# First head pair of a cluster attention: norms, identity products in TensorE's pauses, transfers and masks rearranged

## The chip, the cores and the metric

The kernel runs on one core of a Trainium2 chip. The metric is the device time of one execution in microseconds (us), as the median of three runs. All times below are in us unless they are marked ns. The engines are called TensorE (PE in the views; PEld is its weight load), VectorE (DVE), ScalarE (ACT), GpSimd (POOL) and SyncE (SP, which here only issues transfers).

## The reference

Attention over 2 batches, 8 heads, 768 positions and 64 elements a head, in which a query sees only the keys of its own cluster; two expert layers follow, which the change does not touch.

```python
def _attn_ref(q, k, v, centroids) -> np.ndarray:
    ...
    q_n = q / (np.linalg.norm(q, axis=-1, keepdims=True) + 1e-06)
    k_n = k / (np.linalg.norm(k, axis=-1, keepdims=True) + 1e-06)
    c_n = centroids / (np.linalg.norm(centroids, axis=-1, keepdims=True) + 1e-06)
    q_assign = np.argmax(np.einsum('bhsd,hcd->bhsc', q_n, c_n), axis=-1)
    k_assign = np.argmax(np.einsum('bhsd,hcd->bhsc', k_n, c_n), axis=-1)
    mask = q_assign[:, :, :, None] == k_assign[:, :, None, :]
    scores = scale * np.matmul(q, k.transpose(0, 1, 3, 2))
    scores = np.where(mask, scores, -1000000000.0)
    scores = scores - np.max(scores, axis=-1, keepdims=True)
    attn = np.exp(scores)
    attn = attn / (np.sum(attn, axis=-1, keepdims=True) + 1e-09)
    return np.matmul(attn, v).astype(np.float32)

def reference(**kwargs):
    ...
    x = _moe_ref(x=x, **moe_kwargs)
    return _moe2_ref(x=x, **moe2_kwargs)
```

## The kernel before

The order of the instructions is written out by hand: each engine works through its queue in the order of the program, and a semaphore holds an instruction until its operands are there.

Heads go in eight pairs. A loop of 96 steps (`s`), 12 to a pair, does the attention: a step takes 128 queries of one head against 768 keys (`st_scores`, score buffer `sps`, one of the two buffers of tag S), reduces the row maximum on VectorE (`st`), takes the exponential on ScalarE (`st_exp`, `pr`), and three steps later transposes `pr` on TensorE (`tps`) and copies it out on ScalarE (`pt`). The preparation of the next pair is spread over the steps by a table (`plan`, `prep`); that of pair 0, and part of that of pair 1, stands ahead of the loop, and the change lies there.

Ahead of the loop, for pair 0:

- `load_qk(0)` loads q and k of the pair into `first`; `first_copy` sorts them into `nat`; `raw_pe` transposes them in four parts (q half 0, q half 1, k half 0, k half 1) into `rawps`, and `raw_act` copies each part to `raw`.
- `prep_centroids` makes the norms of the centroids from `cnat` on VectorE, with a square root on ScalarE and two steps that improve it, and writes the normed centroids `cexp`; `prep_cblk` transposes them (`cps`) and copies them to `cblk`.
- `assign_pe` multiplies `raw` by `cblk` (`asps`), `assign_act` copies the result (`sc`), `argmax_pe` transposes it (`scps`), and `argmax_0` to `argmax_3` find each position's cluster on VectorE (`mx`, `eq`, `eq`, `mx`, `oh`).
- `mask_first` transposes the one-hot clusters `oh` in 24 small pieces (`mps`). ScalarE copies the keys' part and VectorE scales the queries' part into rows 64 to 79 of `UA` (head 0) and `UB` (head 1).
- The scores are made in float32 from two parts of each operand: `first_hi` makes the high part (in `UA`, both heads stacked), `first_lo` the low one. Nine transfers inside the core's memory (192 KB each, L502 to L516) bring the parts of each head together in `UA`, `UB`, `VA` and `VB`. A step multiplies first the U tiles and then the V tiles of its head.

For pair 1, `raw_pe`, `raw_act` and `split_first` do the same from `natq` and `natk`; its splits run on GpSimd.

A product or transpose of TensorE loads its stationary operand first (PEld). A float32 product of `nc.tensor.matmul` is issued as two instructions, a transpose as one. `warm` is a 1-column tile on which ScalarE runs an Sqrt at the start and an Exp before the loop, so that the function tables are loaded there.

Of the kernel before, what the change touches and what calls it, by code (L numbers as in the profile page):

```python
# [25 lines left out]
def kernel(  # L26
# [66 lines left out]
    def load_qk(p):  # L93
        b, cc = divmod(p, NPAIR)
        for nm, src in (("q", q), ("k", k)):
            if p:
                t = att_a.tile([P, NT, 2, D], F32, tag="nat" + nm, name="nat" + nm)
                nat[nm, p] = t
                nc.sync.dma_start(t, src[b, 2 * cc:2 * cc + 2].rearrange("h (p t) d -> p t h d", t=NT))
            else:  # L100
                t = att.tile([P, 2, HS], F32R, tag="pr", name="first", bufs=4)
                t = _f(t.rearrange("p a b -> p (a b)")).rearrange("p (h t d) -> p h t d", h=2, d=D)
                nc.sync.dma_start(t, src[b, 0:2].rearrange("h (p t) d -> p h t d", t=NT))
                first[nm] = t
                nat[nm, 0] = nat0[:, "qk".index(nm)]
            if p == 0 and nm == "q":
                nc.sync.dma_start(cnat, centroids.rearrange("h c d -> (h c) d"))
# [29 lines left out]
    nc.scalar.activation(out=warm, in_=warm, func=AF.Sqrt)  # L137
# [5 lines left out]
    def prep_centroids():  # L143
        sq = att_a.tile([P, D], F32, tag="csq", name="csq")
        st = att_a.tile([P, 8], F32, tag="cst", name="cst")
        nc.vector.tensor_tensor(out=sq, in0=cnat, in1=cnat, op=ALU.mult)
        nc.vector.tensor_reduce(out=st[:, 0:1], in_=sq, axis=AX.X, op=ALU.add)
        first_copy(1)
        nc.scalar.activation(out=st[:, 1:2], in_=st[:, 0:1], func=AF.Sqrt)
        nc.vector.tensor_scalar(out=st[:, 1:2], in0=st[:, 1:2], scalar1=1e-30, scalar2=None, op0=ALU.max)  # L150
        for i in (1, 2):
            nc.vector.reciprocal(out=st[:, 3:4], in_=st[:, i:i + 1])
            nc.vector.scalar_tensor_tensor(out=st[:, 3:4], in0=st[:, 0:1], scalar=st[:, 3:4], in1=st[:, i:i + 1],
                                           op0=ALU.mult, op1=ALU.add)
            nc.vector.tensor_scalar(out=st[:, 2 * i:2 * i + 1], in0=st[:, 3:4], scalar1=0.5, scalar2=1e-6 * (i - 1),
                                    op0=ALU.mult, op1=ALU.add)
        nc.vector.reciprocal(out=st[:, 4:5], in_=st[:, 4:5])
        for h in range(2):
            nc.vector.tensor_scalar(out=cexp[:, h, :], in0=cnat, scalar1=st[:, 4:5], scalar2=par[:, h:h + 1],
                                    op0=ALU.mult, op1=ALU.mult)  # L160

    def prep_cblk():
        cps = ps_s("cps")[:, 0, 0:P]
        nc.tensor.transpose(cps, cexp.rearrange("p h d -> p (h d)"), ident)
        nc.vector.tensor_copy(cblk.rearrange("p a b -> p (a b)"), cps)
# [5 lines left out]
    def raw_pe(p, i):  # L171
# [5 lines left out]
        ps = ((ps_t, ps_t, ps_m, ps_a)[i] if p == 0 else ((ps_t, ps_t, ps_a, ps_t)[i] if p == 1 else ps_m))([P, 3, P], "rawps")  # L177
# [9 lines left out]
    def raw_act(p, i):  # L187
        qk, half = divmod(i, 2)
        ps = ps_prep.pop(("raw", i)).rearrange("p j c -> p (j c)")
        sc = SCALE if qk == 0 else 1.0  # L190
        nc.scalar.activation(out=raw_t[p][:, i, :], in_=ps, func=AF.Copy, scale=sc)
# [9 lines left out]
    def raw_split(p, i):  # L201
# [6 lines left out]
        nc.gpsimd.tensor_scalar(out=hi, in0=raw[:, i, :], scalar1=1.0, scalar2=1.0, op0=ALU.mult, op1=ALU.mult)  # L208
# [63 lines left out]

    def mask_first(h):
        U = uv_t[0][h]
        for qk in (1, 0):
# [8 lines left out]
            else:  # L284
                for cs in (slice(0, HS), slice(HS, S)) if h == 0 else (slice(0, S),):
                    nc.vector.tensor_scalar(out=U[64:64 + NC_, 0, cs], in0=ps[:, cs], scalar1=BIG, scalar2=-BIG,
                                            op0=ALU.mult, op1=ALU.add)
# [181 lines left out]
    def first_copy(i):  # L469
        nm = "qk"[i // 2]  # L470
        ts_ = slice(3 * (i % 2), 3 * (i % 2) + 3)
        for h in range(2):
# [3 lines left out]
            elif nm == "q":  # L476
                nc.vector.tensor_copy(dst, src)
# [3 lines left out]
    first_copy(0)  # L481
    prep_centroids()
    first_copy(2)
    first_copy(3)
    for i in range(4):
        raw_pe(0, i)
        raw_act(0, i)
# [6 lines left out]
    def first_lo(qk, halves=(0, 1)):  # L494
        for half in halves:
# [5 lines left out]
    Uk, Wk, Xk, Yk = (_f(t[:, 1, :]) for t in (UA, UB, VA, VB))  # L501
    nc.sync.dma_start(Wq[0:64], Uq[64:128])  # L502
    nc.sync.dma_start(Yq[64:128], Uq[64:128])
    nc.sync.dma_start(Wk[0:64], Uk[64:128])
    nc.sync.dma_start(Yk[0:64], Uk[64:128])
    first_lo(0, (0,))
    prep_cblk()
    first_lo(0, (1,))
    nc.sync.dma_start(Yq[0:64], Xq[64:128])
    nc.gpsimd.dma_start(Xk[0:64], Uk[0:64])  # L510
    assign_pe(0)
    first_lo(1)
    lo_kf = _f(lo_k.rearrange("p a b -> p (a b)"))
    nc.sync.dma_start(Xk[64:128], lo_kf[0:64])
    nc.sync.dma_start(Yk[64:128], lo_kf[64:128])
    nc.sync.dma_start(Xq[64:128], Uq[0:64])  # L516
    prep(0, 3, "a0")
    nc.scalar.activation(out=warm, in_=warm, func=AF.Exp)
    prep(0, 3, "pb")
    for r in range(4, 7):  # L520
        for slot in ("d", "pb"):
            prep(0, r, slot)
    load_v(0)
    for i in range(4):
        raw_pe(1, i)
        raw_act(1, i)
    load_qk(2)
    mask_first(0)
    mask_first(1)
    for i in range(4):  # L530
# [158 lines left out]
    for s in range(NSTEP + 12 + LAG):  # L689
        p, r = divmod(s, 12)  # L690
        if s < NSTEP:
            st_scores(s)
        conv_step(s, 0)
# [931 lines left out]
```

## Time and profile before

| | |
|---|---|
| median of 3 runs | 644.96 us (644.65 to 645.3) |
| the profiled execution, its own time | 644.19 us |
| its span, first to last instruction | 642.5 us |
| outside its span | 1.7 us |
| TensorE busy in the span | 624.0 us (97%) |
| first product of the loop starts at | 18.61 us |
| mean granted TensorE clock | 0.996 |

The span is the time from the first to the last instruction of one execution that was profiled; what lies outside it is start and end of the program. The profiled execution is 0.77 us shorter than the median of the runs. A busy share is an average over stages with different limits; the stage ahead of the loop has to be read by itself.

### The profile page before, as it was taken

The numbers are of one execution on the slowest core, as the hardware profiler recorded it, in microseconds if no ns is written. First come the engines' busy times: TensorE is split into PE (matmuls) and PEld (weight loads), VectorE is DVE, ScalarE is ACT, GpSimd is POOL, SyncE is SP. The second block draws the span as 40 slices with busy tenths as digits, with TensorE's granted clock in tenths as the row PEclk, the third lists the DMA queues.
The fourth block names the chain that finished last, engine by engine and source line by source line (L and its number), as shares of the span: only waits on it lengthen the run. The fifth ranks groups of instructions, "written<-read, shape, count | busy, mean of one in ns | idle before, by whom it ended". The sixth has DMA issues, their size and how long they took to land.

```text
span 642.5 us, 10035 instructions
## 1 busy us (share of the span) xinstructions
PE 624.0 (97%) x3505; PEld 484.2 (75%) x3505; DVE 484.7 (75%) x893; ACT 417.0 (65%) x817; POOL 164.4 (26%) x215
## 2 busy tenths in 40 slices
PE   5999999999999999999999999999999999999994
PEld 3777777677777775888888888878888778688874
DVE  6757868777878754988865888868887748999961
ACT  5798898988888885655454444435445446688860
POOL 3333647463746333400000000000000125005211
PEclk9999999999999999999999999999999999999998
DMA  7766566578766508132014301008421739999930
GB/s 189 193 180 169 138 153 190 150 197 199 200 186 162 174 31 318 67 119 91 23 36 146 100 33 34 33 2 301 178 94 66 267 137 318 372 363 350 369 135 28
DMA packets 66246, 104.26 MB, mean 162 GB/s; under 512 B 27994, under 2 KB 32060, under 8 KB 65810
## 3 DMA queue, kind: packets, MB, share of 16 engines
q1 hardware_dynamic: 62914, 95.36, 47.5%
q0 software_dynamic: 3280, 8.24, 3.9%
q8 instruction: 28, 0.46, 0.3%
q14 instruction: 24, 0.20, 0.1%
HBM read 77.45 MB, written 12.72 MB: 140 GB/s over the span
## 4 chain that ended last, share of the span: by engine, by line
PE 91%; DVE 3%; ACT 2%; DMA 2%; SPq 1%; issue 1%; POOL 0%; POOLq 0%
PE ups L669 20%; PE acc L775 19%; PE sps L371 10%; PE avps L443 10%; PE tps L428 9%; PE hps L1316 7%; PE yps L1347 7%; PE rawps L179 1%; PE hT L1328 1%; PE acc L1208 1%; PE asps L232 1%; ACT pr L389 1%; DMA stg<-in_moe_w_in_dram 1%; DMA first<-in_k_dram 1%; PE scps L244 1%
## 5 line engine op out<-in xcount | busy, mean ns | idle before, releaser
L374 DVE TENSOR_REDUCE st<-sps 128x1 f32<-128x768 f32 x96 | 91.5, 954 | 49.9 <-PE sps L371 49.1
L435 ACT ACTIVATE pt<-tps 128x384 f32<-128x384 f32 x192 | 85.4, 508 | 17.6 <-PE tps L428 16.4
L389 ACT ACTIVATE pr<-sps,st 128x768 f32<-128x768 f32 x96 | 88.0, 917 | 11.5 <-DVE st L374 11.4
L428 PE MATMUL tps<-ident,pr 128*128 128x128 f32 x576 | 79.0, 273 | 0.5 <-ACT pt L435 0.5
L669 PE MATMUL ups<-xh,whii 128*128 128x512 f32 x192 | 74.9, 390 | 0.0
L669 PE MATMUL ups<-xh,wloi 128*128 128x512 f32 x192 | 74.7, 389 | 0.0
L669 PE MATMUL ups<-xl,whii 128*128 128x512 f32 x192 | 74.7, 389 | 0.0
L428 PEld LDWEIGHTS tps<-ident,pr 128*128 128x128 f32 x576 | 67.9, 140 | 5.6 <-ACT pt L435 1.6
L443 PE MATMUL avps<-pt,vnat 128*64 128x384 f32 x384 | 72.1, 498 | 0.0
L775 PE MATMUL acc<-whio,gh 128*128 128x512 f32 x183 | 72.1, 394 | 0.0
L775 PE MATMUL acc<-whio,gl 128*128 128x512 f32 x183 | 71.3, 389 | 0.0
L775 PE MATMUL acc<-wloo,gh 128*128 128x512 f32 x183 | 71.2, 389 | 0.0
L760 ACT ACTIVATE gh<-g 128x512 fp32r<-128x512 f32 x48 | 30.4, 632 | 47.5 <-DVE g L759 47.5
L758 ACT ACTIVATE lk<-ups 128x512 f32<-128x512 f32 x48 | 28.5, 595 | 48.8 <-PE ups L669 43.4
L762 DVE TENSOR_TENSOR gl<-g,gh 128x512 fp32r<-128x512 f32 x48 | 33.2, 691 | 25.2 <-ACT gh L760 25.2
L1048 POOL DMA_INDIRECT xe<-x_scratch,eix x1 | 1.2, 1165 | 189.8 <-DVE eix L1047 189.8
L881 DVE SCALAR_TENSOR_TENSOR ohe<-x,x2Ts 128x512 f32<-128x512 f32 x63 | 43.4, 689 | 1.5
L443 PEld LDWEIGHTS avps<-pt,vnat 128*64 128x64 f32 x384 | 23.4, 136 | 25.5 <-issue 25.1
L759 DVE TENSOR_TENSOR g<-ups,lk 128x512 f32<-128x512 f32 x48 | 33.0, 688 | 12.7 <-ACT lk L758 12.1
L669 PEld LDWEIGHTS ups<-xh,whii 128*128 128x128 f32 x192 | 36.0, 188 | 8.0 <-issue 0.6
L669 PEld LDWEIGHTS ups<-xh,wloi 128*128 128x128 f32 x192 | 36.0, 188 | 7.5
L669 PEld LDWEIGHTS ups<-xl,whii 128*128 128x128 f32 x192 | 36.1, 188 | 7.4
(312 smaller groups left out, 1367.1 us busy)
## 6 DMA issues: line engine op xcount, KB each, us to landing
rawb<-in_moe_w_dram SPq DMA_DIRECT2D x25, 1024.0 KB
rawa<-in_moe_w_dram SPq DMA_DIRECT2D x10, 1024.0 KB
stg<-in_moe_w_in_dram SPq DMA_DIRECT2D x16, 512.0 KB
stg<-in_moe_w_out_dram SPq DMA_DIRECT2D x16, 512.0 KB
x2Ts<-gate_scratch SPq DMA_DIRECT2D x18, 256.0 KB
UB<-UA SPq DMA_DIRECT2D x16, 192.0 KB
vnat<-in_v_dram SPq DMA_DIRECT2D x8, 384.0 KB
rb<-recip_scratch POOLq DMA_DIRECT2D x32, 96.0 KB, 2.8
```

The lines of the kernel that those rows point to most:

```text
L371: nc.tensor.matmul(ps[:, kh, 0:HS], lhsT=t[0:n, 0, qs], rhs=t[0:n, 1, kh * HS:(kh + 1) * HS], start=first, stop=not first)
L374: nc.vector.tensor_reduce(out=st[:, 0:1], in_=ps[:, :, 0:HS], axis=AX.XY, op=ALU.max, negate=True)
L389: nc.scalar.activation(out=pr, in_=ps[:, :, 0:HS], func=AF.Exp, bias=st[:, 0:1], accum_out=sm_t[g][:, 3 * h + j:3 * h + j + 1])
L428: nc.tensor.transpose(ps[:, t, :], pr[:, kh, t * P:(t + 1) * P], ident)
L435: nc.scalar.activation(out=pt[:, 3 * kh:3 * kh + 3, j, :], in_=t_t[s][kh], func=AF.Copy)
L443: nc.tensor.matmul(av_t[g][64 * h:64 * h + 64, :], lhsT=vnat[p][:, h, kt, :], rhs=pt_t[p, half, h][:, kt].rearrange("p j c -> p (j c)"), s ...
L669: nc.tensor.matmul(ps, lhsT=w[:, cc, :], rhs=x[:, blk, cc, :], start=(n == 0), stop=(n == 3 * KD - 1))
L762: nc.vector.tensor_tensor(out=gl, in0=g, in1=_f(gh), op=ALU.subtract)
L775: nc.tensor.matmul(ps, lhsT=a[:, ts_], rhs=w, start=(fc == 0 and n == 0), stop=(fc == NFC - 1 and n == 2))
L881: nc.vector.scalar_tensor_tensor(out=junk[0].rearrange("p t n -> p (t n)"), in0=x2_t[blk, t // 2][:, t % 2, :], scalar=1.0, in1=wgb_t[blk, ...
L1316: nc.tensor.matmul(ps, lhsT=x[:, c, :], rhs=w, start=(n == 0), stop=(n == len(mm) - 1))
L1347: nc.tensor.matmul(ps[:, cs], lhsT=x[:, f, :], rhs=w[:, cs], start=(h == 0 and f == 0 and n == 0), stop=(h == 1 and f == 3 and n == 2))
```

## The change

The change rewrites the stage ahead of the loop, and the first three steps of the loop.

- The centroids are loaded from ScalarE's queue instead of SP's. The square root of their norms is no longer ScalarE's: VectorE halves the bits of the number as a first guess and takes three improving steps instead of two. The table that ScalarE loads at the start is that of Exp, and the second load before the loop is gone.
- All of `first_copy`'s head-0 part is GpSimd's (VectorE did that of q). The copy of `raw` part 1 is VectorE's instead of ScalarE's.
- `warm_pe(n)` multiplies the identity by itself n times into one half of a score buffer (`first_s`); nobody reads the result. It stands in four places (7, 3, 2 and 6 products). The centroids' transpose uses the other half of the same buffer, and so the three products ahead of `assign_pe` wait for VectorE's copy of it (`cblk`).
- Nine transfers become seven: two parts are copied by ScalarE inside the same partitions (L538, L539 after), and `Xq` is issued from ScalarE's queue instead of SP's, where it stood last.
- Of the queries' masks only half 0 is scaled ahead of the loop; half 1 follows in steps 1 and 2 (`mask_query`).
- Of pair 1, parts 0 and 1 stay ahead of the loop; parts 3 and 2 are transposed and copied after the first step's products. Its splits on GpSimd wait for `hold`, a 1-column tile that VectorE writes behind `oh`.

```diff
-                nc.sync.dma_start(cnat, centroids.rearrange("h c d -> (h c) d"))
+                nc.scalar.dma_start(cnat, centroids.rearrange("h c d -> (h c) d"))
...
-    nc.scalar.activation(out=warm, in_=warm, func=AF.Sqrt)
+    nc.scalar.activation(out=warm, in_=warm, func=AF.Exp)
+    hold = const.tile([P, 1], F32, name="hold")
...
-        first_copy(1)
-        nc.scalar.activation(out=st[:, 1:2], in_=st[:, 0:1], func=AF.Sqrt)
-        nc.vector.tensor_scalar(out=st[:, 1:2], in0=st[:, 1:2], scalar1=1e-30, scalar2=None, op0=ALU.max)
-        for i in (1, 2):
+        si = st.bitcast(I32)
+        nc.vector.tensor_single_scalar(si[:, 1:2], si[:, 0:1], 1, op=ALU.logical_shift_right)
+        nc.vector.tensor_scalar(out=si[:, 1:2], in0=si[:, 1:2], scalar1=float(0x1FBD1DF5), scalar2=None, op0=ALU.add)
+        for i, j in ((1, 2), (2, 5), (5, 4)):
...
+    first_s = ps_s("first")
+
     def prep_cblk():
-        cps = ps_s("cps")[:, 0, 0:P]
+        cps = first_s[:, 1, 0:P]
...
+        if p == 0 and i == 1:
+            nc.vector.tensor_scalar(out=raw_t[p][:, i, :], in0=ps, scalar1=sc, scalar2=None, op0=ALU.mult)
+            return
...
-        nc.gpsimd.tensor_scalar(out=hi, in0=raw[:, i, :], scalar1=1.0, scalar2=1.0, op0=ALU.mult, op1=ALU.mult)
+        nc.gpsimd.tensor_scalar(out=hi, in0=raw[:, i, :], scalar1=hold if p == 1 and i == 0 else 1.0, scalar2=1.0,
+                                op0=ALU.mult, op1=ALU.mult)
...
+    mq_t = {}
+
+    def mask_query(h, half):
+        cs = slice(half * HS, (half + 1) * HS)
+        nc.vector.tensor_scalar(out=uv_t[0][h][64:64 + NC_, 0, cs], in0=mq_t[h][:, cs], scalar1=BIG, scalar2=-BIG,
+                                op0=ALU.mult, op1=ALU.add)
...
-                for cs in (slice(0, HS), slice(HS, S)) if h == 0 else (slice(0, S),):
-                    nc.vector.tensor_scalar(out=U[64:64 + NC_, 0, cs], in0=ps[:, cs], scalar1=BIG, scalar2=-BIG,
-                                            op0=ALU.mult, op1=ALU.add)
+                mq_t[h] = ps
+                mask_query(h, 0)
...
-            elif nm == "q":
-                nc.vector.tensor_copy(dst, src)
...
+    wps = first_s[:, 0, 0:P]
+
+    def warm_pe(n):
+        for _ in range(n):
+            nc.tensor.matmul(wps, lhsT=ident, rhs=ident, start=True, stop=True)
+
+    warm_pe(7)
     prep_centroids()
-    first_copy(2)
-    first_copy(3)
     for i in range(4):
+        first_copy(i)
+    for i in range(3):
         raw_pe(0, i)
-        raw_act(0, i)
+    raw_act(0, 0)
+    raw_act(0, 1)
+    prep_cblk()
+    raw_pe(0, 3)
+    raw_act(0, 2)
+    raw_act(0, 3)
+    warm_pe(3)
+    assign_pe(0)
+    warm_pe(2)
     for i in range(4):
         first_hi(i)
...
     nc.sync.dma_start(Wq[0:64], Uq[64:128])
-    nc.sync.dma_start(Yq[64:128], Uq[64:128])
+    first_lo(0)
+    nc.sync.dma_start(Yq[0:64], Xq[64:128])
     nc.sync.dma_start(Wk[0:64], Uk[64:128])
     nc.sync.dma_start(Yk[0:64], Uk[64:128])
-    first_lo(0, (0,))
-    prep_cblk()
-    first_lo(0, (1,))
-    nc.sync.dma_start(Yq[0:64], Xq[64:128])
-    nc.gpsimd.dma_start(Xk[0:64], Uk[0:64])
-    assign_pe(0)
     first_lo(1)
...
-    nc.sync.dma_start(Xq[64:128], Uq[0:64])
     prep(0, 3, "a0")
-    nc.scalar.activation(out=warm, in_=warm, func=AF.Exp)
     prep(0, 3, "pb")
+    nc.scalar.activation(out=VA[0:64, 1, :], in_=Uk[0:64], func=AF.Copy)
+    nc.scalar.activation(out=VB[64:128, 0, :], in_=Uq[64:128], func=AF.Copy)
+    nc.scalar.dma_start(Xq[64:128], Uq[0:64])
...
-    load_v(0)
-    for i in range(4):
+    nc.vector.memset(hold, 1.0)
+    for i in range(2):
         raw_pe(1, i)
         raw_act(1, i)
+    warm_pe(6)
+    load_v(0)
...
+        if s == 0:
+            for i in (3, 2):
+                raw_pe(1, i)
+            for i in (3, 2):
+                raw_act(1, i)
+            for i in (2, 3):
+                split_first(1, i)
+        if 1 <= s < 3:
+            mask_query(s - 1, 1)
```

Three places of the order. TensorE's queue from its first instruction to the masks (`nat_87` is `nat`, `first` in a product's output is the shared score buffer, `oh` is loaded as the stationary operand of the mask transposes); first before, then after the change:

```order
L179 MATMUL rawps<-ident,nat_87 128x128 x12
L164 MATMUL cps<-ident,cexp 128x128
L232 MATMUL asps<-raw,cblk 32x384 x4
L244 MATMUL scps<-ident,sc 128x128 x3
L179 MATMUL rawps<-ident,natq 128x128 x6
L179 MATMUL rawps<-ident,natk 128x128 x6
L280 LDWEIGHTS oh
```

```order
L496 MATMUL first<-ident 128x128 x7
L182 MATMUL rawps<-ident,nat_87 128x128 x9
L167 MATMUL first<-ident,cexp 128x128
L182 MATMUL rawps<-ident,nat_87 128x128 x3
L496 MATMUL first<-ident 128x128 x3
L239 MATMUL asps<-raw,cblk 32x384 x4
L496 MATMUL first<-ident 128x128 x2
L251 MATMUL scps<-ident,sc 128x128 x3
L182 MATMUL rawps<-ident,natq 128x128 x6
L496 MATMUL first<-ident 128x128 x6
L294 LDWEIGHTS oh
```

Eighteen identity products have come in, the centroids' transpose has moved ahead of the last three transposes of pair 0, and the six transposes of `natk` have left this stretch.

ScalarE's queue from the first copies to the loop's first exponentials (`UA<-mps` and `UB<-mps` are the keys' masks, `pr` the exponentials); first before, then after:

```order
L475 ACTIVATE nat_87<-first 128x3x64 x2
L191 ACTIVATE raw<-rawps 128x384 x4
L197 ACTIVATE UA<-raw 128x384 x2
L238 ACTIVATE sc<-asps 128x384
L518 ACT_TABLE_LOAD
L518 ACTIVATE warm<-warm 128x1
L191 ACTIVATE raw<-rawps 128x384 x4
L283 ACTIVATE UA<-mps 16x768
L283 ACTIVATE UB<-mps 16x768
L389 ACTIVATE pr,sm<-sps,st 128x768 x2
```

```order
L488 ACTIVATE nat_87<-first 128x3x64 x4
L197 ACTIVATE raw<-rawps 128x384 x3
L203 ACTIVATE UA<-raw 128x384 x2
L245 ACTIVATE sc<-asps 128x384
L538 ACTIVATE VA<-UA 64x768
L539 ACTIVATE VB<-UA 64x768
L540 DMA VA<-UA 64x768
L197 ACTIVATE raw<-rawps 128x384 x2
L297 ACTIVATE UA<-mps 16x768
L297 ACTIVATE UB<-mps 16x768
L197 ACTIVATE raw<-rawps 128x384 x2
L402 ACTIVATE pr,sm<-sps,st 128x768 x2
```

One copy of `raw` and the table load have left; two copies of 64 rows and a transfer's issue have come in behind `sc`, and two copies of pair 1 now stand between the masks and the first exponential.

SP's queue from the first transfer inside the core's memory to the loads of `v` and of pair 2; first before, then after:

```order
L502 DMA UB<-UA 64x768
L503 DMA VB<-UA 64x768
L504 DMA UB<-UA 64x768
L505 DMA VB<-UA 64x768
L509 DMA VB<-VA 64x768
L514 DMA VA<-lo_k 64x768
L515 DMA VB<-lo_k 64x768
L516 DMA VA<-UA 64x768
L112 DMA vnat<-in_v_dram 128x2x384
```

```order
L528 DMA UB<-UA 64x768
L530 DMA VB<-VA 64x768
L531 DMA UB<-UA 64x768
L532 DMA VB<-UA 64x768
L534 DMA VA<-lo_k 64x768
L535 DMA VB<-lo_k 64x768
L112 DMA vnat<-in_v_dram 128x2x384
```

The transfer that brings the low part of q (`VB<-VA`) has moved from fifth to second place, and the last one, which may not start before that one has been read, has gone to ScalarE's queue.

## Rows read from the trace of the kernel before

**Rows 1.** Page: busy time by engine; the chain that ended last, by engine.

```profile
PE 624.0 (97%) x3505; PEld 484.2 (75%) x3505; DVE 484.7 (75%) x893; ACT 417.0 (65%) x817; POOL 164.4 (26%) x215
...
PE 91%; DVE 3%; ACT 2%; DMA 2%; SPq 1%; issue 1%; POOL 0%; POOLq 0%
```

**Rows 2.** Chain that ended last, 0 to 20 us: start us, us, what.

```profile
1.81 4.57 DMA first<-in_k_dram
...
9.21 1.57 PE asps L232 x8
...
10.80 0.50 ACT sc L238
...
11.35 0.92 PE scps L244 x3
...
12.29 0.57 DVE mx L251
...
14.65 1.25 DVE oh L269
...
15.95 2.73 PE mps L280 x24
18.68 1.25 PE sps L371 x4
```

**Rows 3.** Timeline, 4 to 10 us: start us, us, engine line operation, count.

```profile
4.03 0.61 ACT L475 ACTIVATE nat<-first 128x192 f32<-128x192 f32 x2 [1.70 <-DMA first<-in_q_dram]
...
4.30 0.21 DVE L146 TENSOR_TENSOR csq<-cnat 128x64 f32<-128x64 f32 x1
...
6.40 0.61 ACT L475 ACTIVATE nat<-first 128x192 f32<-128x192 f32 x2 [1.39 <-DMA first<-in_k_dram]
...
6.71 0.69 DVE L159 TENSOR_SCALAR cexp<-cnat,cst,par 128x64 f32<-128x64 f32 x2
...
6.92 2.03 ACT L191 ACTIVATE raw<-rawps 128x384 f32<-128x384 f32 x4
...
8.79 0.28 DVE L165 COPY cblk<-cps 128x128 f32<-128x128 f32 x1
8.85 0.93 ACT L197 ACTIVATE UA<-raw 128x384 fp32r<-128x384 f32 x2
```

**Rows 4.** Timeline of TensorE later: the same operations, and a 128x128 product.

```profile
20.64 0.85 PE L232 MATMUL asps<-raw,cblk 128*32 128x384 f32 x8
...
23.25 0.55 PE L244 MATMUL scps<-ident,sc 128*128 128x128 f32 x3 [0.29 <-ACT sc L238]
...
31.44 0.33 PE L292 MATMUL ohps<-identb,oh 128*128 128x128 bf16 x3
...
521.21 0.69 PE L1055 MATMUL xT<-ident,xe 128*128 128x128 f32 x4
```

**Rows 5.** Timeline: GpSimd at 15 to 16 us; pair 1's last argmax step.

```profile
15.45 0.81 POOL L208 TENSOR_SCALAR UA<-raw 128x384 fp32r<-128x384 f32 x1
...
30.34 0.55 DVE L269 TENSOR_TENSOR oh<-eq,mx 128x384 bf16<-128x384 f32 x1
```

**Rows 6.** SP's wait, two issues; GpSimd's issue; a window (last: PEclk, DMA, GB/s).

```profile
SPq L516 <- DMA VB<-VA: 1.8, 1, 1.8
...
8.49 0.55 SPq L502 DMA_DIRECT2D UB<-UA  x1
...
16.16 0.46 SPq L516 DMA_DIRECT2D VA<-UA  x1
...
VA<-UA POOLq DMA_DIRECT2D x1, 192.0 KB, 4.6
...
10.00:12.00 2.00, 1.37 (x11) 0.65 (x4) 0.47 (x1) 1.18 (x2) 0.76 (x1) 1.00 0.94 203
```

**Rows 7.** Timeline of ScalarE: the loop's first and fourth exponential.

```profile
20.94 0.90 ACT L389 ACTIVATE pr<-sps,st 128x768 f32<-128x768 f32 x1 [2.07 <-DVE st L374]
...
25.63 0.91 ACT L389 ACTIVATE pr<-sps,st 128x768 f32<-128x768 f32 x1
```

More of the change, by code (lines that the diff above doesn't have):

```diff
@@ L154, in prep_centroids @@
                                            op0=ALU.mult, op1=ALU.add)
-            nc.vector.tensor_scalar(out=st[:, 2 * i:2 * i + 1], in0=st[:, 3:4], scalar1=0.5, scalar2=1e-6 * (i - 1),
+            nc.vector.tensor_scalar(out=st[:, j:j + 1], in0=st[:, 3:4], scalar1=0.5, scalar2=1e-6 if j == 4 else 0.0,
                                     op0=ALU.mult, op1=ALU.add)
@@ L176, in raw_pe @@
         src = nat["qk"[qk], p]
-        ps = ((ps_t, ps_t, ps_m, ps_a)[i] if p == 0 else ((ps_t, ps_t, ps_a, ps_t)[i] if p == 1 else ps_m))([P, 3, P], "rawps")
+        ps = ((ps_t, ps_t, ps_m, ps_a)[i] if p == 0 else ((ps_t, ps_t, ps_m, ps_t)[i] if p == 1 else ps_m))([P, 3, P], "rawps")
         for j in range(3):
@@ L475, in first_copy @@
                 nc.scalar.activation(out=dst, in_=src, func=AF.Copy)
-            elif nm == "q":
-                nc.vector.tensor_copy(dst, src)
             else:
                 nc.gpsimd.tensor_scalar(out=dst, in0=src, scalar1=1.0, scalar2=1.0, op0=ALU.mult, op1=ALU.mult)
-    first_copy(0)
+    wps = first_s[:, 0, 0:P]
[3 more added lines that the diff above has]
+    warm_pe(7)
     prep_centroids()
-    first_copy(2)
-    first_copy(3)
     for i in range(4):
+        first_copy(i)
+    for i in range(3):
         raw_pe(0, i)
-        raw_act(0, i)
+    raw_act(0, 0)
[7 more added lines that the diff above has]
+    warm_pe(2)
     for i in range(4):
@@ L492, with first_lo @@
     lo_k = att.tile([P, 2, HS], F32R, tag="pr", name="lo_k", bufs=4)
-    def first_lo(qk, halves=(0, 1)):
-        for half in halves:
+    def first_lo(qk):
+        for half in range(2):
             cs = slice(half * HS, (half + 1) * HS)
@@ L501 @@
     Uk, Wk, Xk, Yk = (_f(t[:, 1, :]) for t in (UA, UB, VA, VB))
+    lo_kf = _f(lo_k.rearrange("p a b -> p (a b)"))
     nc.sync.dma_start(Wq[0:64], Uq[64:128])
-    nc.sync.dma_start(Yq[64:128], Uq[64:128])
+    first_lo(0)
+    nc.sync.dma_start(Yq[0:64], Xq[64:128])
     nc.sync.dma_start(Wk[0:64], Uk[64:128])
     nc.sync.dma_start(Yk[0:64], Uk[64:128])
-    first_lo(0, (0,))
-    prep_cblk()
-    first_lo(0, (1,))
-    nc.sync.dma_start(Yq[0:64], Xq[64:128])
-    nc.gpsimd.dma_start(Xk[0:64], Uk[0:64])
-    assign_pe(0)
     first_lo(1)
-    lo_kf = _f(lo_k.rearrange("p a b -> p (a b)"))
     nc.sync.dma_start(Xk[64:128], lo_kf[0:64])
     nc.sync.dma_start(Yk[64:128], lo_kf[64:128])
-    nc.sync.dma_start(Xq[64:128], Uq[0:64])
     prep(0, 3, "a0")
-    nc.scalar.activation(out=warm, in_=warm, func=AF.Exp)
     prep(0, 3, "pb")
+    nc.scalar.activation(out=VA[0:64, 1, :], in_=Uk[0:64], func=AF.Copy)
+    nc.scalar.activation(out=VB[64:128, 0, :], in_=Uq[64:128], func=AF.Copy)
+    nc.scalar.dma_start(Xq[64:128], Uq[0:64])
     for r in range(4, 7):
@@ L529 @@
     mask_first(1)
-    for i in range(4):
+    for i in range(2):
         split_first(1, i)
```

## The prediction

> **What bounds the kernel now.** I read the page first. TensorE is busy for 97% of the span and carries 91% of the chain that ended last [rows 1], so the loop and the expert layers behind it move with TensorE: what the loop's start gains or loses goes through to the end, unless something in the loop is tied to another clock than the loop's. Nothing the change touches lies behind the loop's third step. So the next view is the chain in order of time up to 20 us [rows 2]. It is not a TensorE chain but a relay: k's load ends at 6.38 (1.81 + 4.57), `asps` begins at 9.21, `sc` at 10.80, `scps` at 11.35, the five argmax steps run from 12.29 to 15.90 (14.65 + 1.25), the mask transposes `mps` from 15.95 to 18.68, then the first scores. Each hand-over is waited for, so here a shorter step is worth its full length.
>
> Two things in this stretch are slower than the same work later. The eight `asps` instructions take 1.57 (chain, to the hand-over) against 0.85 at 20.64, and three `scps` transposes 0.92 against 0.55 [rows 2, 4]. This is TensorE at its lower level, 1.2 GHz; later it runs at 2.4. The column of the granted clock prints 1.00 here too [rows 6], so I trust the durations instead. And `oh` takes 1.25 in pair 0 but 0.55 in pair 1 [rows 2, 5]. What differs is GpSimd, which works on pair 1's splits beside the first (15.45 to 16.26).
>
> **The change part by part, at 2.4 GHz from about 6 us on.** I make the sum in the profiled execution (644.19 = 642.5 span + 1.7 around it; the runs' median, 644.96, lies 0.77 higher) and carry the difference to the median.
>
> *Up to `asps`.* Seven identity products start when `ident` is there (estimate 1.4). Four float32 products later in the kernel take 0.69 for four instructions, two products [rows 4]; taking off one drain of some 0.2, a product is 0.22 to 0.25 at the upper level, about 0.43 at the lower. So the seven fill TensorE to about 4.6, q's transposes follow at once, and the work on q, whose load ended at 4.03 [rows 3], is hardly delayed. The centroid chain on VectorE went from 4.30 to 7.40 [rows 3]. It gains one improving step (three small operations, about 0.64) and a two-operation guess, and loses the hand-over to ScalarE and a copy of q: about 3.8 in all. Its load, one issue earlier on a free queue, should land at 3.5 to 4.2, so `cexp` is ready at 7.3 to 8.0. I take 7.4. The transposes `cps` and then k's last three follow, to 8.0. ScalarE copies three parts of `raw` instead of four (four took 2.03 [rows 3]), the last at 8.5. `cblk` is ready at 8.15, the three identity products take 0.7 behind it, and `asps` starts at 8.85: **-0.35** against 9.21.
>
> *`asps` and `scps`.* -0.70 and -0.37 by the durations above, the hand-overs counted. ScalarE makes k's high parts (0.93 [rows 3]) before `sc`, from 8.5 to 9.45, still ahead of `asps`' end at 9.7. The two identity products behind `asps` end before `sc` does. **-1.07**.
>
> *Argmax.* `hold` keeps GpSimd idle until `oh` is written, so 0.55 instead of 1.25: **-0.70**. Between the ends 0 and 0.70 I take the whole, since [rows 5] is the same instruction with GpSimd idle. What is late instead is GpSimd's split of pair 1: four parts of 1.5 from 13.7 on, the last two not before their copies at 17.3, so to about 20.7. Pair 1 is wanted by the loop's thirteenth step.
>
> *Masks.* 24 transposes took 2.73; at the upper level three take 0.33 [rows 2, 4], one drain of 0.22 and 0.055 each, so 24 take 1.5: **-1.23**. The six identity products ahead end at about 12.7, before `oh` at 13.7, and cost nothing. Half of the queries' scaling leaves too, but it was hidden behind the transposes.
>
> These make -3.35: the first product of the loop at 15.25 instead of 18.61. It and its neighbours then no longer run partly at the lower level: 1.25 for four [rows 2] becomes 1.0, **-0.25**.
>
> *Transfers.* The first product of the V tiles needs `Xq` and `Xk`. Before, SP waited until 16.16 for the low part of q to land, the sixth transfer of the batch that began with the issue at 8.49 [rows 6]; the transfer engines were 0.94 busy from 10 to 12 [rows 6]. Six transfers from about 10.1 to 16.1 are one each 1.0; by the rate in that window, 203 GB/s, 192 KB take 0.97. After the change `Xk` and `Xq` are among the first six of seven, so they land at 15.9, and the V product, ready at 15.7, waits: **+0.2**. The bounds: no wait, or the 4.6 that GpSimd's transfer took from issue to landing [rows 6], which from `Xq`'s issue at 12.6 gives 17.2, +1.5. I take the value of the shared rate. The Trainium skill ("Trainium Kernel Development and Optimization", Key Constraints) says that transfers issued from several queues run on the same 16 engines and that more queues save issue time alone. The busy share agrees. A queue with a rate of its own would land `Xq` near 14.6 and take the 0.2 away.
>
> *Two copies in the loop.* Parts 3 and 2 of pair 1 put six transposes (0.7) between the first and second step's products and two copies (0.5 each by [rows 3]) ahead of the first exponential, which would otherwise wait for its row maximum at 17.4; they end at 17.75: **+0.35**. The copies that leave the stretch ahead were hidden there. The exponential starts at 17.75 instead of 20.94 [rows 7]. The masks' second halves take 0.55 each on VectorE in steps 1 and 2; the second one delays the fourth exponential by some 0.2: 22.7 against 25.63 [rows 7].
>
> Removed with no effect: the second table load (ScalarE had time until the masks). Cover gone: ScalarE's wait for the landing of the low part of q (about 12.0), behind which stand the issue (0.55), two copies of pair 1 (0.5 each) and the masks' copy; the two end at 13.6, and the masks come at 14.25. A landing later than 12.7 would delay the masks.
>
> Sum: -0.35 - 1.07 - 0.70 - 1.23 - 0.25 + 0.2 + 0.35 + 0.15 = **-2.9**. The profiled execution would take 641.3, the median **642.1**.
>
> **The rivals.**
>
> *The clock rises late, about when `mps` comes (1.1 to 1.6 saved).* For it: in the kernel before, stretches of transposes from 11.35 on left `mps` at 0.114 each, the lower level, and only the dense stretch from 15.95 was followed by the upper one. Then the three products ahead of `asps` cost 1.3, `asps` and `scps` save nothing, and 1.3 to 1.8 of the gain goes: **643.4 to 643.9**. Against: seven products and q's transposes fill 1.4 to 6 without a pause.
>
> *Transposes do not hold the clock up (1.4 saved).* Then the identity products raise it, but in the six-transpose and 24-transpose stretches it is low again: `mps` and the first scores give back 1.23 + 0.25: **643.6**. Against: before, the clock came up right behind `mps`, which is transposes alone [rows 2, 4]. The Trainium skill states this rule ("TensorE: Matmul & The Clock Gate", Part 4: PE-mode transpose): a transpose does not count as busy for the clock as a product does. The trace speaks against it so far.
>
> *`Xq` is late (1.6 saved).* ScalarE's transfer behaves as GpSimd's did, 17.2, 1.3 behind the 15.9 of the sum: **643.4**. For it: the engines are full then.
>
> *The loop takes it back (nothing saved).* If pair 1's splits and exchanges, which hardly end earlier while the loop is three earlier, hold the thirteenth step: **645.0**. Against: twelve steps of 1.6 (25.63 less 20.94 over three, [rows 7]) are 19 us from the first product, to 34, and the splits end at 20.7.
>
> *Slower.* The clock stays low until the loop. Then `asps` starts at 9.6 (8.3 + 3 x 0.43), ends at 11.2, `scps` waits for the two products until 12.0, the six transposes and six products end at 16.5 (12.65 + 1.3 + 2.6), after `oh` at 15.9, and `mps` ends at 19.3 instead of 18.7. With the two copies, 0.35: 0.95 more, **645.9**. It decides from the point where the six products end behind `oh`, which they do if the clock is still low at 12.7.
>
> **How the numbers follow.** The forecast has 0.53 (its own range 641.3 to 642.9), the late clock 0.18, the transposes 0.07, the late transfer 0.12, nothing saved 0.05, slower 0.05. A difference of under 0.2% (1.3 us) is about what cannot be told from none. Faster by more: 0.53, and 0.14, 0.05 and 0.10 of the next three, 0.82. Slower 0.05, within 0.2% the other 0.13. The range goes from 640.9 (no wait for transfers, none of the 0.5 in the loop, and `asps` not held by the three products, 0.5) to 643.9, the far end of the late clock; the last two cases stay out.
>
> **What would show it.** In the profile after: `asps` at about 0.87 and starting at 8.6 to 9.2; `mps` at 1.5 for 24; `oh` at 0.55 with GpSimd idle beside it; first score product at 15.0 to 15.7; first exponential near 17.8, fourth near 22.7, and from there each step 2.9 earlier to the end. A clock that rises after 10 us shows in `asps` at 1.5. A wait of the first V product for a transfer beyond 16.5, or a wait of TensorE near the thirteenth step, would show the rivals. Wrong altogether if the loop starts earlier and the end does not move with it.

## The result, and the profile after

The changed kernel takes 652.11 us (median of 4 runs, 651.56 to 652.37) against 644.81 (4 runs, 644.27 to 645.3) of the kernel before on the same chip: ratio 1.0112, 95% interval 1.0095 to 1.013. It is 7.3 slower, where 2.9 less was forecast. The profiled execution has 652.37 and a span of 650.5, 8.0 longer than before.

The page after, its line of busy time ([rows 1]): TensorE is busy for 8.2 more.

```profile
PE 632.2 (97%) x3541; PEld 487.5 (75%) x3541; DVE 483.0 (74%) x898; ACT 417.5 (64%) x815; POOL 165.5 (25%) x216
```

The timeline after, up to the fourth exponential (start us, us, engine, line, operation), beside [rows 2] and [rows 7]:

```profile
9.18 0.85 PE L239 MATMUL asps<-raw,cblk 128*32 128x384 f32 x8
...
10.67 0.55 PE L251 MATMUL scps<-ident,sc 128*128 128x128 f32 x3
...
11.25 0.56 DVE L258 TENSOR_REDUCE mx<-scps 128x24 f32<-128x384 f32 x1 [0.84 <-PE scps L251]
...
12.28 0.52 ACTq L540 DMA_DIRECT2D VA<-UA  x1
...
13.62 0.56 DVE L276 TENSOR_TENSOR oh<-eq,mx 128x384 bf16<-128x384 f32 x1
...
14.23 1.51 PE L294 MATMUL mps<-identb,oh 128*16 128x128 bf16 x24 [1.02 <-DVE hold L544]
...
15.87 0.59 PE L384 MATMUL sps<-UA 80*128 80x384 f32 x2
...
16.85 0.62 PE L384 MATMUL sps<-VA 128*128 128x384 f32 x2 [0.39 <-DMA VA<-UA]
...
17.51 0.96 DVE L387 TENSOR_REDUCE st<-sps 128x1 f32<-128x768 f32 x1 [1.18 <-PE sps L384]
...
18.73 0.90 ACT L402 ACTIVATE pr<-sps,st 128x768 f32<-128x768 f32 x1
...
23.66 0.91 ACT L402 ACTIVATE pr<-sps,st 128x768 f32<-128x768 f32 x1
```

So the stage that the change is about did get shorter: the loop's first product is 2.74 earlier (18.61 before), the fourth exponential 1.97 (25.63). The loop's first row maximum, which began at 17.51, is 2.44 earlier; before:

```profile
19.95 1.82 DVE L374 TENSOR_REDUCE st<-sps 128x1 f32<-128x768 f32 x2 [0.28 <-PE sps L371]
```

To see where this lead goes, take one operation that comes in every step of a later stage and subtract its starts in the two traces. In the first expert layer that is `lk`, ScalarE's copy behind each group of `ups` products. The timeline of ScalarE, the 1st, 5th and 47th `lk` before:

```profile
255.63 0.60 ACT L758 ACTIVATE lk<-ups 128x512 f32<-128x512 f32 x1 [0.17 <-PE ups L669]
...
272.04 0.60 ACT L758 ACTIVATE lk<-ups 128x512 f32<-128x512 f32 x1 [0.48 <-PE ups L669]
...
503.45 0.60 ACT L758 ACTIVATE lk<-ups 128x512 f32<-128x512 f32 x1 [2.02 <-PE ups L669]
```

and after:

```profile
254.96 0.60 ACT L790 ACTIVATE lk<-ups 128x512 f32<-128x512 f32 x1
...
276.19 0.60 ACT L790 ACTIVATE lk<-ups 128x512 f32<-128x512 f32 x1 [1.14 <-PE ups L692]
...
511.27 0.60 ACT L790 ACTIVATE lk<-ups 128x512 f32<-128x512 f32 x1 [2.22 <-PE ups L692]
```

After minus before: -0.67, then +4.15, then +7.82. Three losses of different form: the loop gives back 1.8 of the 2.4 that its first row maximum was early; 4.8 go in one place at the start of the expert layer; 3.7 go evenly over the rest of it. Behind it hardly more is lost (0.2 to the end of the span). (Of the loop's 1.8, 0.6 go in the first twelve steps, where the moved parts of pair 1 and the masks' halves now run; the rest goes in small pieces over the other 84, which I have not followed in this trace.) The second loss, in the timeline after:

```profile
259.64 0.68 DVE L791 TENSOR_TENSOR g<-ups,lk 128x512 f32<-128x512 f32 x1
...
260.37 0.50 PE L692 MATMUL ups<-xh,whii 128*128 128x512 f32 x1 [2.65 <-DVE g L791]
...
261.70 0.63 PE L692 MATMUL ups<-xh,wloi 128*128 128x512 f32 x1
...
264.69 0.53 PE L807 MATMUL acc<-whio,gh 128*128 128x512 f32 x1
```

TensorE stands 2.65 ahead of the third group of `ups`, until VectorE has read the second group (`g`). The same stretch in windows of TensorE (start and end, length, busy time and count, granted clock, DMA share, GB/s):

```profile
252.00:256.00 4.00, 4.00 (x18) 1.00 0.76 269
256.00:260.00 4.00, 1.72 (x8) 1.00 0.08 25
...
261.50:263.00 1.50, 1.50 (x6) 0.52 0.00 0
...
266.00:270.00 4.00, 4.00 (x19) 1.00 0.00 0
```

Behind the stop the granted clock falls to half, that is to 1.2 GHz, and is back by 266; a product takes 0.63 for 0.40 meanwhile. The stop and the clock together are nearly all of the 4.8; the rest is the start of the slow drift.

The slow drift is in the duration of one product, by line from 280 to 500 us (busy us, mean ns), after:

```profile
L692 PE MATMUL ups<-xh,whii 128*128 128x512 f32 x158 | 62.4, 395 | 0.0
```

and before:

```profile
L669 PE MATMUL ups<-xh,whii 128*128 128x512 f32 x160 | 62.3, 390 | 0.0
```

TensorE never waits in either. A product is 5 to 7 ns longer (389 to 396 for `wloi`), and 504 of the 576 `ups` products lie between the 5th and the 47th `lk`: 2.5 to 3.5. The `acc` products with `gl` are 2 ns longer too (389 to 391, 168 of them), 0.3 more. That is the drift.

### The profile page after: what moved, and what is told of

It reads as the page before. It is cut to its first block, busy times and chain, and to the rows that moved or that the text cites. A ratio compares the mean times of both kernels' runs of the same rounds, so it can differ in the third digit from the quotient of the medians.

```text
span 650.5 us, 10107 instructions
## 1 busy us (share of the span) xinstructions
PE 632.2 (97%) x3541; PEld 487.5 (75%) x3541; DVE 483.0 (74%) x898; ACT 417.5 (64%) x815; POOL 165.5 (25%) x216
## 5 line engine op out<-in xcount | busy, mean ns | idle before, releaser
L692 PE MATMUL ups<-xh,whii 128*128 128x512 f32 x192 | 76.5, 399 | 2.6 <-DVE g L791 2.6
L692 PE MATMUL ups<-xh,wloi 128*128 128x512 f32 x192 | 76.7, 399 | 0.0
L692 PE MATMUL ups<-xl,whii 128*128 128x512 f32 x192 | 76.4, 398 | 0.0
```

Of the source, the lines that this page charges most:

```text
L692: nc.tensor.matmul(ps, lhsT=w[:, cc, :], rhs=x[:, blk, cc, :], start=(n == 0), stop=(n == 3 * KD - 1))
```

## The experiments

**Theory A: places.** The change also moves tiles, which no instruction in the profile shows; the places below are those in the programs built from the kernels. The first allocation of a tag decides its PSUM banks. Before, `rawps` came first, so tags T, M and A lay in banks 0 to 3 and the score buffers (S) in 4 to 7; now `first_s` comes first, and S lies in 0 to 3. Behind the loop another pool takes banks 0 and 1 for `ups` groups from the third on, while the first two groups are still in score buffers, the second of them in the one over banks 0 and 1: so the third, in bank 0, must wait for the second's reader. And `hold` is a constant tile of its own, 32 bytes with padding, so that every tile behind it on that side of SBUF moves by 32, the weights of the expert layer (`whii`, `wloi`) among them. **Theory B**: the changed order and the clock of the start cause the loss.

*Back in place, one and both.* `hold` in a second column of `warm`, so that nothing in SBUF moves:

```diff
-    warm = const.tile([P, 1], F32, name="warm")
+    warm2 = const.tile([P, 2], F32, name="warm")
+    warm = warm2[:, 0:1]
...
-    hold = const.tile([P, 1], F32, name="hold")
+    hold = warm2[:, 1:2]
```

> The changed kernel, but hold is the second column of warm's tile, so that no tile behind it moves in SBUF; everything else as changed. Theory A (places): the 32 bytes that hold adds move the first expert layer's weights, and its ups products then take 0.232 each instead of 0.227; without the shift the slow drift through that layer (3.7 us) goes and about 648.4 is measured; the stop of TensorE before the third ups product stays. Theory B (order and clock: the new order at the start, or what it does to the clock, slows the layers): 652, as changed.

Measured: 649.13 (6 runs), ratio to before 1.0051 [1.0034, 1.0067]. The banks as before, by allocating pair 0's four `rawps` ahead of `first_s`:

```diff
+    raw0_ps = [f([P, 3, P], "rawps") for f in (ps_t, ps_t, ps_m, ps_a)]
     first_s = ps_s("first")
...
-        ps = ((ps_t, ps_t, ps_m, ps_a)[i] if p == 0 else ((ps_t, ps_t, ps_m, ps_t)[i] if p == 1 else ps_m))([P, 3, P], "rawps")
+        ps = raw0_ps[i] if p == 0 else ((ps_t, ps_t, ps_m, ps_t)[i] if p == 1 else ps_m)([P, 3, P], "rawps")
```

> The changed kernel, but the four PSUM tiles of pair 0's transposes are allocated ahead of the shared score buffer, so that the score buffers lie in banks 4 to 7 as before; same instructions in the same order. Theory A (places): the third ups product, in bank 0, no longer waits for the first two, which lie in a score buffer; the stop of 2.7 us and the fall of the clock behind it go, together 4.8: about 647.3. Theory B (order and clock): 652.

Measured: 648.42 (5 runs), 1.0047 [1.0032, 1.0061]. Both edits:

> The changed kernel with both: hold in warm's tile, and the banks as before. Theory A (places): both losses go and what the start gained is left, less what the attention loop loses on the way (2.4 at its first step, 0.7 at its end): 642.4 to 644.1, 643.6 if the loop's loss has a cause of its own. Theory B (order and clock): 652.

Measured: 643.81 (10 runs, 643.35 to 644.52), **0.9977 [0.9968, 0.9987]**. With both places restored the changed kernel is 1.2 faster than before. In the traces each loss goes with its own edit. With `hold` moved the stop stays (timeline) and the products behind it take 389 to 390 again (by line, 280 to 500 us):

```profile
261.39 0.50 PE L693 MATMUL ups<-xh,whii 128*128 128x512 f32 x1 [3.05 <-DVE g L792]
...
L693 PE MATMUL ups<-xh,whii 128*128 128x512 f32 x160 | 62.3, 390 | 0.0
```

With the banks moved the stop is gone and the drift stays:

```profile
L693 PE MATMUL ups<-xh,whii 128*128 128x512 f32 x157 | 62.0, 395 | 0.0
```

By the ratios the edits give back 0.61% and 0.65% alone and 1.35% together, so within their intervals they add up.

*Each place alone, in the kernel before.* An unused constant tile of 32 bytes, and one score buffer allocated first:

```diff
+    const.tile([P, 8], F32, name="pad")
```

> The kernel before, with an unused tile of 32 bytes in SBUF ahead of everything that lies on its left side; no instruction changes. Theory A (places): the same drift as in the changed kernel, 3.7 us in the first expert layer, perhaps some in the attention loop: 648.5. Theory B (order and clock): 644.8, no change.

```diff
-        cps = ps_s("cps")[:, 0, 0:P]
+        cps = cps_s[:, 0, 0:P]
...
+    cps_s = ps_s("cps")
```

> The kernel before, with one edit: the score buffer that the centroids' transpose uses is allocated ahead of all other PSUM tiles, so the score buffers lie in banks 0 to 3 as in the changed kernel; instructions and their order stay. Theory A (places): the third product group of the first expert layer waits for the first one's reader, TensorE stands some 2.6 us and the clock falls behind it: 4 to 5 us later from there on, 649 to 650, with nothing changed ahead of the expert layer. Theory B (the changed start and its clock are the cause): 644.8 to 645.3.

Measured: 648.85, 1.0058 [1.004, 1.0077] with the unused tile, and 650.29, 1.0072 [1.0049, 1.0096] with the score buffer first. An unused tile costs 3.8; both are A's. The second has another stop in the loop's profile (1.56 at 176), and the same wait at the third group:

```profile
263.58 0.79 PE L670 MATMUL ups<-xh,whii 128*128 128x512 f32 x1 [3.08 <-DVE g L760]
```

Here the products took 0.63 for longer behind the stop, to 268.9, and from the 1st to the 5th `lk` this profile lost 6.1 instead of 4.8.

*What of the place counts.* 64 bytes, then 128, in place of 32:

> The kernel before with an unused constant tile of 64 bytes in place of the 32 of the earlier run: what lies behind it moves by 64 bytes. If the place counts by its remainder to 64 (32 bytes moved operands off it, 64 move them back): no drift in the first expert layer, 644.6 to 645.5. If any shift slows these products, or the additional tile itself does: about 648.8, as with 32.

Measured: 650.37, 1.0082 [1.0059, 1.0105].

> The kernel before with an unused constant tile of 128 bytes: what lies behind it moves by 128, where moves of 32 and of 64 made the ups products of the first expert layer slower (395 ns for 389, a drift of 4 us). If the place counts by its remainder to 128: products at 389 and the time as before, 644.6 to 645.5. If not: products at 395 or so and 648.5 to 650.5.

Measured: 650.6, 1.01 [1.0079, 1.0121]. My idea that the remainder to 64 or to 128 decides fell both times. (The medians rose by 5.6 and 6.1; from the 5th to the 47th `lk` the two profiles lost 4.2 and 4.5. The rest I have not followed.) The tile that counts could be told: 32 bytes ahead of `whii` and `wloi` alone.

```diff
             wip[0] = pool("wi", "left")
+            wip[0].tile([P, 8], F32, name="pad")
```

> The kernel before with 32 unused bytes ahead of the weights' split tiles of the expert layer alone (the high and low parts that the ups products load): only these move, and the tiles behind the attention's release ahead of them, the constants and everything of the attention stay where they were. If the place of the weights that TensorE loads sets the pace of the ups products: 395 ns and a drift of 3.5 to 4 us over the layer as with the constant tile, nothing lost ahead of it, 648.0 to 649.0. If it is another tile's place (the staging buffers, the raw chunks, the constants): products at 389 and 644.3 to 645.2.

Measured: 649.16, 1.0065 [1.004, 1.009]. By line, 280 to 500 us:

```profile
L669 PE MATMUL ups<-xh,wloi 128*128 128x512 f32 x157 | 62.1, 396 | 0.0
L669 PE MATMUL ups<-xh,whii 128*128 128x512 f32 x157 | 62.0, 395 | 0.0
...
L776 PE MATMUL acc<-wloo,gh 128*128 128x512 f32 x158 | 61.5, 389 | 0.0
```

The products that load the moved weights are slower by 6 to 7; that with `wloo`, which did not move, is at 389. Why 395 stays open. One rival is untested: in the program of the kernel before all these weights and their moving operands start at places with the same remainder to 256 (224), and in the slow versions `whii` and `wloi` alone have another (0, 32 or 96). So a remainder to 256 or more could decide, or one shared with the moving operand; a shift by 256 was not run.

**What the loop takes back.** The profile of the kernel with both places as before is of one of its slower executions (644.35). Its loop ends no earlier than before: between the 65th row maximum (1.94 early) and the 69th (0.10 early) TensorE stood:

```profile
175.57 0.55 PE L184 MATMUL rawps<-ident,natq 128*128 128x128 f32 x3 [1.59 <-ACT raw L199]
```

*The changed kernel, both places as before, without the 18 identity products* (`warm_pe` loops over `range(0)`):

> The changed kernel with both places as before, and without its 18 identity products: the new order alone. At the start the forecast's terms for the clock come back: asps at 1.5, scps at 0.9, mps at 2.7, first exponential 1.5 to 2.5 later than with them (18.7), that is 20.2 to 21.2. Theory C (the loop is tied to transfers and GpSimd, which take away what TensorE gains beyond about 1 us): the time moves by less than that, 644.5 to 645.3. Theory D (what the start gains goes through to the end): 645.3 to 646.3.

Measured: 646.26 (12 runs, 644.13 to 648.54), 1.0018 [1.0004, 1.0032]. The number is D's, but the profile (an execution of 644.23) is C's: the first row maximum was 0.91 early, and the end of the loop 0.06. Since the twelve times lie so far apart, one more execution was profiled:

> A second look at the kernel without identity products: its twelve times went from 644.1 to 648.5, eight of them at 646 or above, and the profile on record is of one at 644.23 in which the lead of 0.9 ended as 0.06. If the slow ones are the stop near 172 to 178 us, a profile at 646 or above shows 1.3 to 2 us lost there; at 644 it shows none. Rival: the slow ones lose it at the start, by the clock or a late transfer.

This one took 645.57 and differs in two ways. First, the clock. TensorE in the first profile:

```profile
11.20 0.90 PE L253 MATMUL scps<-ident,sc 128*128 128x128 f32 x3 [0.58 <-ACT sc L247]
...
15.12 2.73 PE L296 MATMUL mps<-identb,oh 128*16 128x128 bf16 x24 [1.74 <-DVE warm L546]
```

and in the second profile:

```profile
14.51 1.51 PE L296 MATMUL mps<-identb,oh 128*16 128x128 bf16 x24 [2.36 <-DVE warm L546]
```

Here the upper level came by itself before `scps` (0.55), and the loop started 2.37 early, as with the identity products. Without them, when the clock rises differs between executions of one kernel. Second, the lead ended in a stop:

```profile
175.51 0.49 ACT L199 ACTIVATE raw<-rawps 128x384 f32<-128x384 f32 x1 [2.88 <-POOL VB L218]
...
176.06 0.55 PE L184 MATMUL rawps<-ident,natq 128*128 128x128 f32 x3 [1.76 <-ACT raw L199]
```

The loop's 65th row maximum was still 1.63 early, the 69th 1.63 late. More than the stop was lost, since the clock fell behind it here as well (windows of TensorE as above):

```profile
177.00:178.50 1.50, 1.50 (x9) 0.54 0.94 203
```

ScalarE's copy into `raw` waits for the last of the previous pair's splits on GpSimd, and GpSimd had stood ahead of them for `recip_scratch`, a 3 KB row of sums. That row is issued from SP behind loads of later data. SP and GpSimd in the kernel before:

```profile
157.95 1.97 SPq L112 DMA_DIRECT2D vnat<-in_v_dram  x1
...
161.00 0.32 SPq L704 DMA_DIRECT2D recip_scratch<-rrow  x1
...
165.24 1.10 POOL L414 DMA_DIRECT2D rb<-recip_scratch  x2 [1.49 <-DMA recip_scratch<-rrow]
```

and in the second profile without identity products:

```profile
154.66 4.51 SPq L112 DMA_DIRECT2D vnat<-in_v_dram  x1
...
160.57 0.34 SPq L738 DMA_DIRECT2D recip_scratch<-rrow  x1
...
165.28 1.10 POOL L429 DMA_DIRECT2D rb<-recip_scratch  x2 [3.16 <-DMA recip_scratch<-rrow]
```

SP reaches the load of `vnat` 3.3 earlier and is held in it for 4.51 instead of 1.97; the row of sums, which ScalarE has written 1.6 earlier, goes out only 0.4 earlier, and GpSimd goes on at the same time as before. So GpSimd moves here with the transfers, not with TensorE.

*The early split*: the last of the four splits one step earlier, ahead of the work that waits for `rb`. With both places as before:

```diff
-            (0, "a0", raw_split, 0), (1, "a0", raw_split, 1), (2, "a0", raw_split, 2), (3, "a0", raw_split, 3),
+            (0, "a0", raw_split, 0), (1, "a0", raw_split, 1), (2, "a0", raw_split, 2), (2, "a0", raw_split, 3),
```

> The changed kernel with both places as before, and the last of a pair's four splits on GpSimd queued one step earlier, ahead of the weighting and splitting of the attention result, for pairs 2 to 5. In the profile of the kernel with both places as before, ScalarE waited 2.71 us for this split in the step at 172 us and TensorE stood 1.59 us, and 1.8 us of lead went. Theory C (this wait is where the lead goes): no such wait there, the lead of 1.9 holds to the end: 642.0 to 643.0. Rival: the transfers of these stages set the time, and another wait takes its place: 643.6 to 644.2.

Measured: 643.09 (12 runs, 642.43 to 645.16), **0.9972 [0.996, 0.9984]**, the lowest median. In its profile (an execution of 642.68) there is no such wait, and the lead of the loop's end (1.45) goes unchanged through the expert layer; its 47th `lk`, against 503.45 before:

```profile
501.97 0.60 ACT L792 ACTIVATE lk<-ups 128x512 f32<-128x512 f32 x1 [2.01 <-PE ups L694]
```

The interval overlaps that without the edit (0.9968 to 0.9987), so in the time its worth is not shown. The traces that speak for it are of one execution each, and in this one the row of sums also went out 2 earlier; but the last split ended 3.1 ahead of the copy, more than that. The same edit in the kernel before:

> The kernel before, with the one edit of the earlier run: the last of a pair's four splits on GpSimd queued one step earlier for pairs 2 to 5. The stop of TensorE near 172 to 178 us was seen with a lead (1.3 to 1.8 us, three kernels) and also without one (1.56, the kernel with the score buffers first), not in the profile of before. Theory C (the stop comes when the work on TensorE runs ahead of GpSimd there): before has no lead, so the edit is worth little, 644.3 to 644.9. Theory E (the stop comes by chance in some executions of any of these kernels): the median hardly moves either, but the executions at 645.5 to 647.5 of before, a quarter of them, go away.

Measured: 645.05, 1.0005 [0.9996, 1.0015]: no gain without a lead, as C says and E allows. E's sign did not come: 5 of the 12 executions are at 645.5 or above (3 of 22 of the kernel before beside them), and the profile has another stop, 0.87 at 180.6. But C is not shown either: the stop near 175 came in four of the five profiles with the old order of splits that were early by 0.68 or more at the 65th row maximum, not in that of after, and once in a kernel that was 0.5 late there (the score buffer first). What brings it stays open. And without the identity products:

> The changed kernel with both places as before, with the early split, and without the 18 identity products. Against the same kernel with them (643.09) this prices the clock with the stop in the loop out of the way: theory D, now (with that stop gone the start's lead goes through): the row maximum of the first step 1.5 later, as in the two profiles, and the time 644.2 to 645.0. Theory C (other waits of the loop still take the lead away): 643.1 to 643.9.

Measured: 644.33 (12 runs, 641.85 to 645.16), 0.9993 [0.998, 1.0005], in D's range. Against 0.9972 the products are worth 0.21% (about 0.04 to 0.38, if the two intervals are combined), some 1.35 of the 1.5 by which they move the first row maximum in the profiles: with that stop out of the way most of the lead goes through. Yet two of the twelve, 641.85 and 642.1, are faster than every execution with the products.

## Why the prediction was wrong

**The step that failed is the first paragraph's**: "Nothing the change touches lies behind the loop's third step." The forecast followed instructions, and none behind the third step changed. But a new first allocation moved the score buffers' banks, and a new constant moved the expert layer's weights by 32 bytes; both are paid 240 us later (4.8 and 3.7), and undoing both turns 1.0112 into 0.9977. No rival named it. The slower rival placed its loss at the start, where none is.

**The sentence ahead of it**, that what the loop's start gains goes through to the end "unless something in the loop is tied to another clock", has its exception at work: of 2.4 at the first row maximum, 1.2 arrive in the median with both places restored, and none in that kernel's profile. So even without the two places the forecast of 2.9 was more than twice too high. The rival "The loop takes it back" had the mechanism (splits of the next pair on GpSimd hold TensorE) but sought it at the thirteenth step and for pair 1. It is near 175, where the transfers hold GpSimd.

**The start, term by term**, against the forecast:

- *Up to `asps`*: 9.18, not 8.85; -0.03 instead of -0.35. `cexp` came at 7.55, inside my range, but `cblk` and the three products took until 9.2.
- *`asps` and `scps`*: from `asps` to the first argmax step 2.07 (9.18 to 11.25) against 3.08: -1.01, forecast -1.07.
- *Argmax*: from there to `oh`'s end 2.93 against 3.61: -0.68, forecast -0.70; `oh` itself 0.56 with GpSimd idle.
- *Masks*: 24 transposes 1.51, forecast 1.5; from their start to the first product 1.64 against 2.66, -1.02 instead of -1.23. But a slow `mps` is no fixed part of the kernel before: in its variants with unchanged start (five with a tile or buffer moved, one with a split earlier) `mps` took 1.51 in four profiles of six. In those four the first V product waited for its transfer instead (0.79 to 0.93), and the first exponential came only 0.3 to 0.45 earlier than in [rows 7].
- *Transfers*: `Xq` landed at 16.8, not 15.9. Issued from ScalarE at 12.28 it took some 4.6, the price of GpSimd's transfer in [rows 6]; the rival's 17.2 from an issue at 12.6 had the right duration. I took the shared rate from one window. The V product waited 0.39 for it, forecast 0.2; it was no more because the first product came at 15.87 instead of 15.25. In the three profiles with identity products and one or both places restored, but the old splits, the first product began at 15.64 to 15.74 and V still at 16.81 to 16.89: here the landing, not the relay, sets the time. The Trainium skill's statement that queues share the 16 engines ("Trainium Kernel Development and Optimization", Key Constraints) fits these 4.6: a queue of its own brought no earlier landing.
- *Copies in the loop*: the first exponential stands 0.26 behind its row maximum (18.47 to 18.73; forecast 0.35), the fourth 0.24 further behind (forecast 0.15). By the forecast's own terms the first was to come at 17.89 (20.94 less 3.05), not at 17.75.
- *The first score products*: the U part took 0.59 for 0.95, so the -0.25 had its cause; with the longer wait for `Xq` in between, the row maximum came 1.64 behind the first product instead of 1.34.

**The clock.** That the identity products raise it early held in all five profiles that have them (`asps` 0.85; 1.77 to 2.14 in the three without). The rival by which transposes do not hold it up did not come: `mps` took 1.51, and the first score products behind these 24 transposes ran at the upper level (0.59). Beyond what I had: in the kernel before with the early split, what ran between `asps` and a fast `mps` was transposes alone.

```profile
9.10 1.51 PE L232 MATMUL asps<-raw,cblk 128*32 128x384 f32 x8 [0.58 <-DVE cblk L165]
11.23 0.90 PE L244 MATMUL scps<-ident,sc 128*128 128x128 f32 x3 [0.63 <-ACT sc L238]
11.93 1.48 PE L179 MATMUL rawps<-ident,natq 128*128 128x128 f32 x6
13.21 1.48 PE L179 MATMUL rawps<-ident,natk 128*128 128x128 f32 x6
15.83 1.51 PE L280 MATMUL mps<-identb,oh 128*16 128x128 bf16 x24 [1.14 <-DVE oh L269]
```

The Trainium skill ("TensorE: Matmul & The Clock Gate", Part 4: PE-mode transpose) says that a transpose does not count as busy for the clock as a product does; these rows speak against it, unless the `asps` products ahead of them brought the rise, which no run here separates.

## What to carry to other kernels

A new tile, even one that nothing reads, and a new first use of a buffer are changes to the whole program: compare where all tiles lie before and after, ask which later pool takes over those banks and who reads them last, and put small tiles into columns that exist. A lead at the start is worth only what the tightest other clock behind it lets through; find the engines that stand for transfers, and see how far ahead of TensorE they are. When a trace loses time, subtract the starts of one repeated operation in both traces: a jump is a wait, a slope is a duration.

## What the hardware showed

- Products of 128x512 whose weights lie 32, 64 or 128 bytes further on took 394 to 397 ns for 389 to 390, over a whole layer, with no wait in the trace: some 4 us. These runs show a dependence on the place, not its reason. The Trainium skill ("SBUF — State Buffer", SBUF: two separate sides) says that TensorE's ports there never wait on another engine; the traces agree (0.0 idle beside these products), so the difference is of another kind.
- A stop of 2.65 cost about 4.8, since the clock fell behind it. Two stops of the same length in the loop differed in this: behind 1.76 (without the identity products) the granted clock was 0.54, behind 1.77 (banks as before) it stayed at 1.00.
- One issue on SP, the same load, took 1.97 or 4.51: an issue can be held, and what stands behind it on the queue is held with it.
- Without the identity products the upper level came at different times in two executions of one program: behind `mps` in one, ahead of `scps` in the other.
